# Moving weight preparation to other visits, and the first expert splits and products into attention, in a fused attention and two-expert kernel

## The chip, the core and the metric

The kernel runs on one core of a Trainium2 chip. TensorE (PE in the profile) multiplies matrices and loads its stationary operand on a track of its own (PEld), VectorE (DVE), ScalarE (ACT) and GpSimd (POOL) work on tiles, and SyncE (SP) issues most of the DMAs. Each engine runs its own instructions in the order in which the program hands them over. The metric is the device time of one execution in microseconds; lower is better.

## What is computed

The inputs are 4 batches of 8 heads, 576 positions, head size 64. Attention with a decay bias gives 2304 tokens of 512 numbers, and two dense experts follow, one behind the other.

```
scores = scale * q @ k.T + min(-(cum_i - cum_j), 0), causal      # cum: running sum of max(s, 0)
attn   = exp(scores - max) / (sum + 1e-9)
x      = attn @ v, as 2304 x 512
h      = max(x @ w_in, 0);        x = (h * h) @ w_out             # w_in 512 x 2048
h      = max(x @ w1, x @ w2, x @ w3);  out = h @ w_out            # w1, w2, w3 512 x 768
```

All of it is float32. The experts get the precision out of products of a shorter type: each operand is split into a high and a low part, and each product is made as three (high x high, high x low, low x high).

## The kernel before

**Attention** runs over 16 head pairs with 9 units each (units 0 to 143; N is 144). A loop over steps n emits, at each step, one stage of several units: ORDER lists the stages with their distances. Scores (u_s, two steps ahead) go to PSUM, u_max (L531, DVE) takes the row maximum, u_exp (L545, ACT) the exponential, u_t (L590, L597, PE) transposes blocks and the row sums into a PSUM tile, w_cp (L556, L558, DVE) takes reciprocals of the sums, u_et (L617 to L622, ACT) copies the blocks out, w_pv (L642, PE) multiplies by v, w_out_ (L653, DVE) copies the result to xT, and w_px (L658, POOL) scales it by the reciprocals, which take a way through DRAM. A head pair has two windows: w_pv is called for the first with units 0 to 3, for the second with units 4 to 8.

**The changeover.** The first products of the first expert are already made in attention. first_split(kk) splits a quarter of the first 512 tokens (ACT makes the high part, L665, DVE the low part, L666), for kk of 0 to 3 at steps 136, 138, 140 and 142. first_products makes 2 x 12 products (L672) into two PSUM banks ("first", which take the place of the tile "pair") at 3 per step from step 144 on, between the stages of the last units. Then experts() splits the same 512 tokens once more into its own tiles xs, and starts.

**The experts** run over tokens in chunks. The first expert has nine visits: chunks 0 to 3 (512, 512, 512, 384 tokens) with the first 8 of 16 blocks of the hidden size (visits 0 to 3), chunk 4 (384) with all 16 (visit 4), and chunks 3, 2, 1, 0 with the other 8 (visits 5 to 8). main1 lists its steps: a step "h" makes 12 products for a block (L672), whose result ACT and DVE turn into a split hidden block (L777 ACT, L778 DVE, L780 ACT, L781 DVE), and a step "x" two blocks later multiplies that by w_out into four PSUM banks with 12 products (L798). At the end of a visit the four banks are copied out (L808 DVE for two of them, L810 ACT), and in visits 0 to 3 stored to DRAM as partial sums. The next visit takes the same four banks one step later. Splits xs of the next visit's tokens are made in the last steps of a visit. The second expert follows in 6 chunks of 384 (L838, L879).

**Weights.** There are 56 weight tiles: 32 of the first expert ("in", "out"), 24 of the second (18 "w", 6 "out2"). Each must be prepared by a job (w_job): two loads on SP, DVE instructions L340, L344, L348, L351, (L355), a high part on ACT (L360) and a low part on DVE (L363, for which adder says GpSimd or DVE; in the experts L355 and L363 are DVE's). The class Slots plans the jobs: pump() is called once per step, advances open jobs, and starts one if a weight is needed soon (SOON) or if the pace allows. There are 24 slots in SBUF. Tiles of the second expert may also be prepared early ("early"): with no slot the job's result goes to a tile "spare", is stored to DRAM (keep, L366, SP), and is fetched into a slot 6 steps before its use by a DMA of GpSimd's queue (w_bring, L379). Early jobs begin only from step 80 (EARLY_FROM), in the middle of visit 4, and no faster than one in PACE_EARLY 2.4, counted in steps of 512 tokens.

**The plan that comes out.** By steps of main1 (a visit of 8 blocks is 16 steps; visit 4 is steps 62 to 93 with its last products at step 97), jobs begin at steps 1 to 25, one in two steps; none from 26 to 62, when all slots are taken; then "in" 13 to "out" 15 from 63 to 79, then 8 "w" tiles straight into slots from 81 to 98, and 16 early jobs from 102 to 149. The 16 kept tiles are fetched at steps 162 to 183.

Of the kernel before, what the change touches and what calls it, by code (L numbers as in the profile page):

```python
# [9 lines left out]
F32R = mybir.dt.float32r  # L10
# [3 lines left out]
ALU = mybir.AluOpType  # L14
# [4 lines left out]
HELD_BACK = 3  # L19
# [3 lines left out]
PUMP_FROM = 9  # L23
PUMP_END = 0
PRE = 2
PRE_X = 8
PRE_AT = 0
PRE_N = 3
PUMP_U = (0, 2, 3, 4, 5, 7)
WA_BUFS = 3  # L30
DELAY_ATT = (2, 6, 2, 2, 2, 2, 4, 0, 1, 1)
# [3 lines left out]
SOON = 6  # L35
SOON_KEPT = 6
PACE_EARLY = 2.4
EARLY_FROM = 80
RR = 2
LAG = 2  # L40
MAX_OPEN = 3
# [39 lines left out]
class Slots:  # L81
# [8 lines left out]
    def __init__(self, steps, make, bring, early, room):  # L90
        self.steps = steps
        self.uses = {}
        for n, ids in enumerate(steps):
            for i in ids:
                self.uses.setdefault(i, []).append(n)
        self.make, self.bring, self.early, self.room = make, bring, early, dict(room)
        self.free = []
        self.held = {}
        self.open = []
        self.kept = set()  # L100
        self.coming = set()
        self.pos = 0
        self.clock = 0.0
        self.last = -100.0
        self.pace = PACE_ATT
        self.delays = DELAY_ATT
        self.most = ADV_ATT
        self.idle_from = None

    def add(self, tiles):  # L110
        self.free += tiles
# [52 lines left out]
    def start(self):  # L164
        for n in range(self.pos, len(self.steps)):
            for i in self.steps[n]:
                if i in self.held or i in self.coming:
                    continue
                kept = i in self.kept
                if n - self.pos > (SOON_KEPT if kept else SOON) and (kept or self.clock - self.last < self.pace):  # L170
                    return False
                if not kept and not self.can_open():
                    return False
                if not self.free and not self.evict(n):
                    return False
                self.fill(i)
                return True
        return False

    def pump(self, time):  # L180
        self.clock += time
        done = 0
        for job in list(self.open):
            while job in self.open and self.clock >= job.ready and done < self.most:
                if not self.step(job):
                    break
                done += job.at > 2
        if not self.start() and self.idle_from is not None and self.pos >= self.idle_from and \
                self.clock - self.last >= PACE_EARLY and self.can_open():
            going = [job.i for job in self.open]  # L190
            i = next((i for i in self.early if i not in self.held and i not in self.kept and i not in going), None)
# [23 lines left out]
def kernel(  # L215
# [15 lines left out]
    nc = tc.nc  # L231
    P = 128
    D = v_tail.shape[2]
    S = qT.shape[2]
# [17 lines left out]
    def f32(ap):  # L252
        return ap.bitcast(F32)
# [406 lines left out]

    three = ((0, 0), (0, 1), (1, 0))

    def split_x(t0, n, kk, high, low):
        src = xT[:, kk, t0:t0 + n]
        nc.scalar.copy(out=high[:, 0:n], in_=src)  # L665
        nc.vector.tensor_tensor(out=low[:, 0:n], in0=src, in1=f32(high[:, 0:n]), op=ALU.subtract)  # L666
        return high, low

    def h_products(hps, x, n, w):
        for kk in range(KD):  # L670
# [5 lines left out]

    first_x = {}

    def first_split(kk):
        if kk < HELD_BACK:  # L680
            high, low = (slots_a[-1 - kk][:, i, :] for i in range(2))
        else:
            high, low = (hp.tile([P, S], F32R, tag=n, name=n)[:, 0:512] for n in ("xk", "xq"))
        first_x[kk] = split_x(*chunks1[0], kk, high, low)

    def first_products():
        for m in range(PRE):
# [2 lines left out]
    def attention():  # L690
# [10 lines left out]
        for n in range(-span, N + span + 1):  # L701
# [10 lines left out]
            for op, d in ORDER:  # L712
# [8 lines left out]
                        wfn[op](*wins[n + d])  # L721
                elif 0 <= n + d < N:
                    fns[op](n + d)
            if n == N:
                phQ.close()
                banks.extend(psum(ctx, "first", 2, [P, 512]))
            if PRE and n >= N - PRE_X and (n - N + PRE_X) % 2 == 0 and (n - N + PRE_X) // 2 < KD:
                first_split((n - N + PRE_X) // 2)
            if n >= N - PRE_AT:
                for _ in range(PRE_N):  # L730
                    next(pre, None)
# [3 lines left out]
    def experts():  # L735
# [2 lines left out]

        slots.delays, slots.most, slots.pace = DELAY, ADV, PACE
        adder[0] = nc.vector  # L740
        slots.idle_from = EARLY_FROM
        slots.add(slots_a[-HELD_BACK:] + [sl_p.tile([P, 2, 512], F32R, name=f"slb{i}") for i in range(SLOTS_B)])

        def xsplit(t0, n, kk):
# [209 lines left out]
```

## Time and profile before

| | us |
|---|---|
| time, median of 3 runs (lowest, highest) | 896.93 (896.42, 897.15) |
| the profiled execution's own time | 896.98 |
| its span, first to last instruction | 895.2 |
| PE busy | 855.9 (96%) |
| DVE busy | 514.3 (57%) |
| ACT busy | 332.2 (37%) |
| POOL busy | 66.9 (7%) |

The profile is of one execution. The 1.8 us between its time and its span lie outside of the instructions. Attention takes up to about 179 us, the first expert from there to about 580, the second up to the end. A busy PE is 96% of the span as the profile models it; where the products of a stretch stand at their even pitch, only a shorter program would help, and where a row shows idle time before it, something was late.

### The profile page before, as it was taken

The numbers are of one execution on the slowest core, as the hardware profiler recorded it, in microseconds if no ns is written. First come the engines' busy times: TensorE is split into PE (matmuls) and PEld (weight loads), VectorE is DVE, ScalarE is ACT, GpSimd is POOL, SyncE is SP. The second block draws the span as 40 slices with busy tenths as digits, with TensorE's granted clock in tenths as the row PEclk, the third lists the DMA queues.
The fourth block names the chain that finished last, engine by engine and source line by source line (L and its number), as shares of the span: only waits on it lengthen the run. The fifth ranks groups of instructions, "written<-read, shape, count | busy, mean of one in ns | idle before, by whom it ended". The sixth has DMA issues, their size and how long they took to land.

```text
span 895.2 us, 14075 instructions
## 1 busy us (share of the span) xinstructions
PE 855.9 (96%) x5446; PEld 730.0 (82%) x5446; DVE 514.3 (57%) x1079; ACT 332.2 (37%) x729; POOL 66.9 (7%) x79
## 2 busy tenths in 40 slices
PE   5999888899899999998999999999999999999998
PEld 3555555577688899997998888899999999999997
DVE  6788797868886333788888777633223131312211
ACT  5788887843333223323333333311112120212111
POOL 2133333310000000000000000110000000000000
PEclk9999999999999999999999999999999999999999
DMA  4454545212321020432425355950000000000001
GB/s 144 152 151 126 177 125 166 86 57 94 125 88 47 1 83 1 142 95 94 130 69 196 116 190 184 318 151 1 13 24 1 36 1 36 1 25 12 12 24 36
DMA packets 45267, 79.00 MB, mean 88 GB/s; under 512 B 7568, under 2 KB 17360, under 8 KB 45200
## 3 DMA queue, kind: packets, MB, share of 16 engines
q1 hardware_dynamic: 42884, 69.70, 24.3%
q0 software_dynamic: 2304, 8.39, 3.1%
q8 instruction: 43, 0.70, 0.3%
q14 instruction: 24, 0.20, 0.1%
q10 hardware_dynamic: 12, 0.01, 0.0%
HBM read 60.84 MB, written 17.22 MB: 87 GB/s over the span
## 4 chain that ended last, share of the span: by engine, by line
PE 75%; DVE 14%; ACT 6%; issue 4%; DMA 1%; DVEq 0%; ACTq 0%
PE banks L838 17%; PE banks L798 16%; PE first L838 8%; PE banks L879 8%; PE first L672 8%; PE banks L672 8%; PE pairs L642 4%; PE pairs L590 3%; DVE e L531 2%; PE pair L508 2%; DVE st L351 2%; PE pairs L508 2%; DVE r L778 2%; ACT hh L780 2%; ACT et L619 2%
## 5 line engine op out<-in xcount | busy, mean ns | idle before, releaser
L798 PE MATMUL banks<-hh,sl 128*128 128x512 f32 (+1 forms) x840 | 187.1, 371 | 4.4 <-DVE pt L808 1.8
L798 PEld LDWEIGHTS banks<-hh,sl 128*128 128x128 f32 x840 | 153.9, 189 | 27.7 <-DVE pt L808 2.2
L838 PE MATMUL banks<-xs,sl 128*128 128x384 f32 x720 | 128.7, 334 | 0.0
L838 PEld LDWEIGHTS banks<-xs,sl 128*128 128x128 f32 x720 | 125.1, 188 | 0.0
L780 ACT CAST hh<-r 128x512 fp32r<-128x512 f32 (+1 forms) x80 | 46.2, 578 | 152.8 <-DVE r L778 152.8
L672 PE MATMUL banks<-xs,sl 128*128 128x512 f32 (+1 forms) x420 | 92.0, 367 | 0.0
L672 PE MATMUL first<-xs,sl 128*128 128x512 f32 (+1 forms) x396 | 87.2, 368 | 4.4 <-DVE xs L666 3.2
L545 ACT ACTIVATE e<-e,nm 128x128 f32<-128x128 f32 (+2 forms) x144 | 83.5, 582 | 11.9 <-DVE nm L531 11.5
L672 PEld LDWEIGHTS banks<-xs,sl 128*128 128x128 f32 x420 | 76.7, 188 | 9.9
L672 PEld LDWEIGHTS first<-xs,sl 128*128 128x128 f32 x396 | 72.3, 188 | 13.9 <-DVE xs L666 3.5
L781 DVE TENSOR_TENSOR hh<-r,hh 128x512 fp32r<-128x512 f32 (+1 forms) x80 | 51.1, 639 | 51.5 <-ACT hh L780 50.2
L854 DVE TENSOR_TENSOR r<-banks,r 128x384 f32<-128x384 f32 x54 | 30.1, 557 | 78.5 <-PE banks L838 78.0
L879 PE MATMUL banks<-sl,hh 128*128 128x512 f32 (+1 forms) x342 | 74.9, 378 | 0.0
L879 PEld LDWEIGHTS banks<-sl,hh 128*128 128x128 f32 x342 | 61.8, 188 | 11.8
L858 ACT CAST hh<-r 128x384 fp32r<-128x384 f32 x36 | 18.5, 513 | 138.4 <-DVE r L854 138.4
L590 PEld LDWEIGHTS pairs<-identF,e 64*128 64x128 f32 x800 | 33.4, 139 | 30.6 <-ACT et L619 23.2
L590 PE MATMUL pairs<-identF,e 64*128 64x64 f32 x800 | 41.4, 230 | 16.8 <-ACT et L619 16.5
L642 PEld LDWEIGHTS pairs<-et,xv 128*64 128x64 f32 (+1 forms) x448 | 27.8, 135 | 31.2 <-ACT e L545 8.3
L642 PE MATMUL pairs<-et,xv 128*64 128x320 f32 (+4 forms) x448 | 52.7, 367 | 0.0
L838 PE MATMUL first<-xs,sl 128*128 128x384 f32 x288 | 52.0, 335 | 0.0
L838 PEld LDWEIGHTS first<-xs,sl 128*128 128x128 f32 x288 | 50.3, 188 | 0.5
L854 DVE TENSOR_TENSOR r<-first,r 128x384 f32<-128x384 f32 x18 | 10.0, 558 | 67.3 <-PE first L838 67.3
(104 smaller groups left out, 1116.1 us busy)
## 6 DMA issues: line engine op xcount, KB each, us to landing
st<-in_w_out_dram SPq DMA_DIRECT2D x44, 256.0 KB
st<-in_w_dram SPq DMA_DIRECT2D x36, 256.0 KB
st<-in_w_in_dram SPq DMA_DIRECT2D x32, 256.0 KB
keep_w<-spare SPq DMA_DIRECT2D x10, 512.0 KB
xk<-in_kT_dram SPq DMA_DIRECT2D x16, 288.0 KB
xq<-in_qT_dram SPq DMA_DIRECT2D x16, 288.0 KB
out_dram<-ob SPq DMA_DIRECT2D x17, 256.0 KB
xv<-in_v_main_dram SPq DMA_DIRECT2D x16, 256.0 KB
```

The lines of the kernel that those rows point to most:

```text
L508: nc.tensor.matmul(b[:, j, 0:w], lhsT=d["xq"][rows(j), w - P:w], rhs=d["xk"][rows(j), 0:w], start=True, stop=False)
L545: nc.scalar.activation(out=e_u[u][:, 0:w], in_=e_u[u][:, 0:w], func=ACTF.Exp, scale=-1.0, bias=st.pop(n), accum_out=sums[p, win][:, col:co ...
L590: nc.tensor.transpose(t[:, h, at * D:(at + 1) * D], e_u[v][rows(h), k * P:(k + 1) * P], identF[rows(h), rows(h)])
L642: nc.tensor.matmul(pv[rows(j), f:(W0, W1)[w]], lhsT=xv[0:kr, j, k, :], rhs=rhs, start=(k == 0), stop=(k == last))
L672: nc.tensor.matmul(hps[:, 0:n], lhsT=w[:, wp, kk * P:(kk + 1) * P], rhs=x[kk][xp][:, 0:n], start=(kk == 0 and c == 0), stop=(kk == KD - 1 ...
L780: nc.scalar.copy(out=hh[:, 0, 0:n], in_=r[:, 0:n])
L781: nc.vector.tensor_tensor(out=hh[:, 1, 0:n], in0=r[:, 0:n], in1=f32(hh[:, 0, 0:n]), op=ALU.subtract)
L798: nc.tensor.matmul(xacc[d][:, 0:n], lhsT=w[:, wp, d * P:(d + 1) * P], rhs=hh[:, xp, 0:n], start=(m == 0 and c == 0), stop=(end and c == 2))
L838: nc.tensor.matmul(pj[j][:, 0:n], lhsT=w[:, wp, kk * P:(kk + 1) * P], rhs=xs[kk][xp][:, 0:n], start=(kk == 0 and c == 0), stop=(kk == KD - ...
L854: nc.vector.tensor_tensor(out=r[:, 0:n], in0=p[:, 0:n], in1=r[:, 0:n], op=ALU.max)
L858: nc.scalar.copy(out=hh[:, 0, 0:n], in_=r[:, 0:n])
L879: nc.tensor.matmul(po[:, 0:hi - lo], lhsT=hs[ci, f][:, hp_, t * P:(t + 1) * P], rhs=w[:, wp, lo:hi], start=(c == 0), stop=(c == 3 * NF2 - 1))
```

## The change

The change does four things.

- Early jobs may begin in any step but those of visits 0, 1 and 4 (EARLY_NOT_IN); before, from step 80 on. As the plan comes out, 8 early jobs ("w" 0,0 to 1,2) now begin at steps 36 to 59, in visits 2 and 3; "in" 13 to "out" 15 stay at 63 to 79; no job begins from 80 to 93; 16 early jobs begin at 94 to 143. So all 24 tiles of the second expert go through DRAM (24 stores and 24 fetches, before 16), and the fetches begin at step 154.
- Weights that are needed more than 24 steps ahead (FAR) are begun at PACE_FAR 3 rather than 1.5: at steps 12, 15, 18, ... 33 rather than 11, 13, 15, ... 25.
- The four first splits move to steps 114, 123, 132 and 139 (PRE_X 30, 21, 12, 5), and the DVE half of each comes one step behind its ACT half.
- The first products begin at step 143 rather than 144 (PRE_AT 1), 5 per step rather than 3.

```diff
-PRE_X = 8
-PRE_AT = 0
-PRE_N = 3
+PRE_X = (30, 21, 12, 5)
+PRE_AT = 1
+PRE_N = 5
...
-EARLY_FROM = 80
+EARLY_NOT_IN = (0, 1, 4)
+FAR = 24
+PACE_FAR = 3
...
-                if n - self.pos > (SOON_KEPT if kept else SOON) and (kept or self.clock - self.last < self.pace):
+                pace = self.pace if n - self.pos <= FAR else max(self.pace, PACE_FAR)
+                if n - self.pos > (SOON_KEPT if kept else SOON) and (kept or self.clock - self.last < pace):
                     return False
...
-        if not self.start() and self.idle_from is not None and self.pos >= self.idle_from and \
+        if not self.start() and self.pos in self.idle and \
                 self.clock - self.last >= PACE_EARLY and self.can_open():
...
-    def first_split(kk):
-        if kk < HELD_BACK:
-            high, low = (slots_a[-1 - kk][:, i, :] for i in range(2))
-        else:
-            high, low = (hp.tile([P, S], F32R, tag=n, name=n)[:, 0:512] for n in ("xk", "xq"))
-        first_x[kk] = split_x(*chunks1[0], kk, high, low)
+    def first_split(kk, low):
+        if not low:
+            if kk < HELD_BACK:
+                first_x[kk] = tuple(slots_a[-1 - kk][:, i, :] for i in range(2))
+            else:
+                first_x[kk] = tuple(hp.tile([P, S], F32R, tag=n, name=n)[:, 0:512] for n in ("xk", "xq"))
+        (high if not low else low_of)(*chunks1[0], kk, *first_x[kk])
...
-            if n == N:
+            if n == N - PRE_AT:
                 phQ.close()
                 banks.extend(psum(ctx, "first", 2, [P, 512]))
-            if PRE and n >= N - PRE_X and (n - N + PRE_X) % 2 == 0 and (n - N + PRE_X) // 2 < KD:
-                first_split((n - N + PRE_X) // 2)
+            for kk in range(KD):
+                for later in range(2):
+                    if n == N - PRE_X[kk] + later:
+                        first_split(kk, later)
...
-        slots.idle_from = EARLY_FROM
+
+        slots.idle = set(range(len(steps)))
+        for i, step in enumerate(main1):
+            if step[1] in EARLY_NOT_IN:
+                slots.idle.discard(i)
```

The new functions high and low_of are the two halves of split_x.

PE at the end of attention, before: the 24 first products (L672) stand in portions of 3, 9 and 12, the last of them behind the last product with v (L642).

```order
L672 MATMUL first_2787<-sl_86,sl_67 128x512 x3
L590 MATMUL pairs_90<-identF,e_154 128x64 x10
L597 MATMUL pairs_90<-identF,sm_2698 5x64 x2
L672 MATMUL first_2787<-sl_85,sl_67 128x512 x3
L672 MATMUL first_2787<-sl_84,sl_67 128x512 x3
L672 MATMUL first_2787<-xk,sl_67 128x512
L672 MATMUL first_2787<-xq,sl_67 128x512
L672 MATMUL first_2787<-xk,sl_67 128x512
L642 MATMUL pairs_91<-et_2757,xv 64x320 x6
L642 MATMUL pairs_91<-et_2757,xv 64x192 x2
L642 MATMUL pairs_91<-et_2757,xv 64x64 x2
L672 MATMUL first_2788<-sl_86,sl_68 128x512 x3
```

PE there after the change (L672 has become L680, L642 L645); five products already stand ahead of the 16 transposes that come before these rows, and five more end and begin around the ten transposes.

```order
L680 MATMUL first_2767<-xk,sl_67 128x512
L593 MATMUL pairs_90<-identF,e_154 128x64 x10
L600 MATMUL pairs_90<-identF,sm_2703 5x64 x2
L680 MATMUL first_2767<-xq,sl_67 128x512
L680 MATMUL first_2767<-xk,sl_67 128x512
L680 MATMUL first_2768<-sl_86,sl_68 128x512 x3
L680 MATMUL first_2768<-sl_85,sl_68 128x512 x3
L680 MATMUL first_2768<-sl_84,sl_68 128x512 x3
L680 MATMUL first_2768<-xk,sl_68 128x512
L680 MATMUL first_2768<-xq,sl_68 128x512
L680 MATMUL first_2768<-xk,sl_68 128x512
L645 MATMUL pairs_91<-et_2757,xv 64x320 x6
```

All 24 first products now stand ahead of the last product with v, which was ahead of 12 of them.

DVE at the end of visit 4, before: up to the copies of the visit's banks (L808), job instructions stand between the hidden blocks (L778, L781).

```order
L778 SCALAR_TENSOR_TENSOR r<-first_2787,r 128x384
L781 TENSOR_TENSOR hh<-r,hh 128x384
L363 TENSOR_TENSOR sl_78<-wa,sl_78 128x512
L340 TENSOR_SCALAR wa<-st 128x512
L344 SCALAR_TENSOR_TENSOR st<-st,wa 128x512
L348 TENSOR_SCALAR wa<-st 128x512
L351 SCALAR_TENSOR_TENSOR st<-st,wa 128x512
L355 TENSOR_TENSOR wa<-st 128x512
L778 SCALAR_TENSOR_TENSOR r<-first_2788,r 128x384
L781 TENSOR_TENSOR hh<-r,hh 128x384
L340 TENSOR_SCALAR wa<-st 128x512
L344 SCALAR_TENSOR_TENSOR st<-st,wa 128x512
```

DVE there after the change (L778 has become L793, L808 L823, L666 L670).

```order
L793 SCALAR_TENSOR_TENSOR r<-first_2768,r 128x384
L796 TENSOR_TENSOR hh<-r,hh 128x384
L793 SCALAR_TENSOR_TENSOR r<-banks_2865,r 128x384
L796 TENSOR_TENSOR hh<-r,hh 128x384
L670 TENSOR_TENSOR xs<-xT,xs 128x384 x2
L793 SCALAR_TENSOR_TENSOR r<-banks_2866,r 128x384
L796 TENSOR_TENSOR hh<-r,hh 128x384
L793 SCALAR_TENSOR_TENSOR r<-first_2767,r 128x384
L796 TENSOR_TENSOR hh<-r,hh 128x384
L793 SCALAR_TENSOR_TENSOR r<-first_2768,r 128x384
L796 TENSOR_TENSOR hh<-r,hh 128x384
L823 COPY xT<-banks_2868 128x384
```

No job instruction is left in the last six hidden blocks ahead of the copies.

DVE at the end of visit 0, before: ahead of the two copies of the visit's banks (L808).

```order
L363 TENSOR_TENSOR sl_82<-wa,sl_82 128x512
L348 TENSOR_SCALAR wa<-st 128x512
L351 SCALAR_TENSOR_TENSOR st<-st,wa 128x512
L355 TENSOR_TENSOR wa<-st 128x512
L340 TENSOR_SCALAR wa<-st 128x512
L344 SCALAR_TENSOR_TENSOR st<-st,wa 128x512
L778 SCALAR_TENSOR_TENSOR r<-first_2788,r 128x512
L781 TENSOR_TENSOR hh<-r,hh 128x512
L363 TENSOR_TENSOR sl_83<-wa,sl_83 128x512
L348 TENSOR_SCALAR wa<-st 128x512
L351 SCALAR_TENSOR_TENSOR st<-st,wa 128x512
L355 TENSOR_TENSOR wa<-st 128x512
```

DVE there after the change.

```order
L366 TENSOR_TENSOR sl_82<-wa,sl_82 128x512
L343 TENSOR_SCALAR wa<-st 128x512
L347 SCALAR_TENSOR_TENSOR st<-st,wa 128x512
L351 TENSOR_SCALAR wa<-st 128x512
L354 SCALAR_TENSOR_TENSOR st<-st,wa 128x512
L358 TENSOR_TENSOR wa<-st 128x512
L793 SCALAR_TENSOR_TENSOR r<-first_2768,r 128x512
L796 TENSOR_TENSOR hh<-r,hh 128x512
L823 COPY pt<-banks_2868 128x512
L823 COPY pt<-banks_2870 128x512
L366 TENSOR_TENSOR sl_83<-wa,sl_83 128x512
```

From the start of the first expert up to the copies, six job instructions fewer stand in DVE's queue, which is one job's worth; the low part of "in" 8 (sl_83) has come behind the copies.

## Rows read from the trace of the kernel before

**Rows 1.** Stretches: us; busy (instructions) of PE, PEld, DVE, ACT, POOL; PEclk, DMA share, GB/s.

```profile
300.00:320.00 20.00, 20.00 (x93) 16.96 (x92) 6.39 (x10) 5.69 (x10) 0.00 (x0) 1.00 0.00 0
400.00:420.00 20.00, 17.70 (x101) 17.01 (x99) 17.27 (x33) 6.42 (x14) 0.00 (x0) 1.00 0.25 87
```

**Rows 2.** Timeline of PE around 416: start us, us, engine, line, count [idle before <-releaser].

```profile
416.06 1.20 PE L672 MATMUL first<-xs,sl 128*128 128x384 f32 x6
...
422.06 1.48 PE L672 MATMUL first<-xs,sl 128*128 128x384 f32 x5 [3.20 <-DVE xs L666]
...
426.70 2.24 PE L672 MATMUL first<-xs,sl 128*128 128x384 f32 x12
428.78 2.24 PE L798 MATMUL banks<-hh,sl 128*128 128x384 f32 x12
...
436.64 2.24 PE L672 MATMUL banks<-xs,slb 128*128 128x384 f32 x12
```

**Rows 3.** Timeline of DVE, the splits that PE waited for.

```profile
421.46 1.02 DVE L666 TENSOR_TENSOR xs<-xT,xs 128x384 fp32r<-128x384 f32 x2
```

**Rows 4.** A short stretch, columns as in rows 1.

```profile
422.00:426.00 4.00, 3.94 (x14) 3.94 (x15) 3.35 (x8) 1.42 (x3) 0.00 (x0) 0.58 0.29 102
```

**Rows 5.** DVE by line and form, 345 to 470 us: busy us, mean ns | idle before.

```profile
L781 DVE TENSOR_TENSOR hh<-r,hh 128x384 fp32r<-128x384 f32 x26 | 14.5, 559 | 15.1 <-ACT hh L780 15.1
L351 DVE SCALAR_TENSOR_TENSOR st<-st,wa 128x512 f32<-128x512 uint32 x18 | 12.5, 694 | 0.6
...
L340 DVE TENSOR_SCALAR wa<-st 128x512 uint32<-128x512 uint32 x18 | 7.6, 421 | 0.0
```

**Rows 6.** Timeline of PE at the end of visit 0.

```profile
236.41 2.88 PE L672 MATMUL banks<-xs,sl 128*128 128x512 f32 x12
239.13 0.92 PE L798 MATMUL banks<-hh,sl 128*128 128x512 f32 x3
...
243.98 2.20 PE L672 MATMUL banks<-xs,sl 128*128 128x512 f32 x9
```

**Rows 7.** Timeline of DVE at the end of visit 0, the two copies.

```profile
241.07 1.28 DVE L808 COPY pt<-banks 128x512 f32<-128x512 f32 x2
```

**Rows 8.** Timeline of PE, last head pairs.

```profile
157.34 0.71 PE L590 MATMUL pairs<-identF,e 64*128 64x64 f32 x16 [1.20 <-ACT et L619]
...
170.87 0.28 PE L590 MATMUL pairs<-identF,e 64*128 64x64 f32 x2 [0.37 <-ACT e L545]
171.78 1.13 PE L508 MATMUL pairs<-xk,xq 64*128 64x512 f32 x4 [0.64 <-DVE nm L531]
```

**Rows 9.** Timeline of DVE, the first of the four splits.

```profile
170.45 0.93 DVE L666 TENSOR_TENSOR sl<-xT,sl 128x512 fp32r<-128x512 f32 x1 [0.76 <-ACT sl L665]
```

**Rows 10.** Timeline of PE at the changeover.

```profile
180.16 0.71 PE L590 MATMUL pairs<-identF,e 64*128 64x64 f32 x16 [1.54 <-ACT et L619]
180.80 0.96 PE L672 MATMUL first<-sl,sl 128*128 128x512 f32 x3
181.69 0.52 PE L590 MATMUL pairs<-identF,e 64*128 64x64 f32 x10
...
184.47 2.42 PE L642 MATMUL pairs<-et,xv 128*64 128x320 f32 x20
...
193.17 2.79 PE L798 MATMUL banks<-hh,sl 128*128 128x512 f32 x11 [0.23 <-DVE hh L781]
```

**Rows 11.** Timeline of DVE at the changeover.

```profile
187.01 0.49 DVE L653 COPY xT<-pairs 128x320 f32<-128x320 f32 x1 [3.44 <-PE pairs L642]
187.41 3.72 DVE L666 TENSOR_TENSOR xs<-xT,xs 128x512 fp32r<-128x512 f32 x4
...
192.43 0.69 DVE L781 TENSOR_TENSOR hh<-r,hh 128x512 fp32r<-128x512 f32 x1 [0.69 <-ACT hh L780]
```

**Rows 12.** Line L658, 184 to 192 us: durations min/median/max, first and last start.

```profile
L658 POOL TENSOR_TENSOR xT<-xT,px x3: 870/917/1033, 184.8 to 189.7; 128x320 f32<-128x320 f32 x2, 128x256 f32<-128x256 f32 x1
```

**Rows 13.** A stretch of the fetches, columns as in rows 1.

```profile
560.00:580.00 20.00, 20.00 (x90) 16.54 (x90) 14.21 (x24) 6.28 (x12) 4.22 (x8) 1.00 1.00 330
```

More of the change, by code (lines that the diff above doesn't have):

```diff
@@ L107, in __init__ @@
         self.most = ADV_ATT
-        self.idle_from = None
+        self.idle = ()
     def add(self, tiles):
@@ L661, with high, low_of, split_x @@
     three = ((0, 0), (0, 1), (1, 0))
[L663 to L667, printed above, removed]
+    def high(t0, n, kk, hi, lo):
+        nc.scalar.copy(out=hi[:, 0:n], in_=xT[:, kk, t0:t0 + n])
+    def low_of(t0, n, kk, hi, lo):
+        nc.vector.tensor_tensor(out=lo[:, 0:n], in0=xT[:, kk, t0:t0 + n], in1=f32(hi[:, 0:n]), op=ALU.subtract)
+    def split_x(t0, n, kk, hi, lo):
+        high(t0, n, kk, hi, lo)
+        low_of(t0, n, kk, hi, lo)
+        return hi, lo
     def h_products(hps, x, n, w):
```

## The prediction, as it was put on record

> **What bounds the kernel now.** I read the 20-us stretches first. In the experts PE is busy all the time in most of them [rows 1]; the exceptions are what a plan can give back. So I went to the timeline of PE and compared the pitch of its steps. Undisturbed, a step of 12 products takes 2.08 us with 384 tokens (428.78 to the row before it, [rows 2]) and 2.72 us with 512 (236.41 to 239.13, [rows 6]), 0.227 us for one product. Three places fall out of that pitch.
>
> The largest is the end of visit 4: from 416.06 to 436.64 PE gets through six steps in 20.58 us, where six at 2.08 are 12.48. So 8.1 us are lost there [rows 2]. Its longest wait is 3.20 us for DVE's splits of the next visit's tokens, which DVE reached at 421.46 [rows 3]. DVE was not waiting for anyone; it was busy 17.27 of 20 us in that stretch, and its rest is the pause of each hidden block between L778 and L781, 15.1 us for 26 blocks [rows 1, 5]. A part of the 8.1 us is clock: after PE had been nearly idle, the granted clock was 0.58 in the next 4 us, a mix of the two levels 1.2 and 2.4 GHz [rows 4]. The six steps include that, and the wait for the copies at the visit's end.
>
> The second is the end of visit 0: a step begins at 239.13 and the next at 243.98, 4.85 us instead of 2.72, so 2.1 us are lost [rows 6]. DVE came to the copies of the visit's banks only at 241.07 [rows 7]; the products wait for them.
>
> The third is the end of attention, where PE waits 0.9 to 1.5 us in each head pair for a copy of ACT, which stands behind DVE's sums (1.20 and 1.54 us, [rows 8, 10]).
>
> **Part 1, the early jobs (weights).** One job costs DVE four instructions like L351 at 0.69 us and two like L340 at 0.42: 3.6 us [rows 5]. A hidden block of 384 tokens costs L778 and L781 at about 0.56 each and the pause of 0.58: 1.7 us [rows 5]. Before, jobs begin from step 63 at one per 2.25 steps, 4.7 us of PE: 3.6 + 1.125 x 1.7 = 5.5 us of DVE by these sums. DVE falls behind by up to 0.8 us a job, and some 14 jobs lie ahead of the splits and copies at the visit's end. After, 8 of them begin, the last at step 79, and their last instruction stands at step 86; then 11 steps or 23 us follow with only hidden blocks (six at 1.7 us, 10 us) and the splits, and a lag of 8 x 0.8 = 6.4 us is worked off there. So the whole 8.1 us should go, the slow clock with them. Bounds: 5 us if some lag is left, 8.1 if none; I take 8.1, as the order shows no job instruction among the last six blocks.
>
> The moved jobs go to visits 2 and 3, where DVE was busy 6.39 of 20 us [rows 1]. There they come one in three steps: with 512 tokens 8.2 us of PE against 3.6 + 1.5 x 2.1 = 6.7 of DVE (a block of 512 is three times 0.69, [rows 11]); with 384 tokens 6.2 against 3.6 + 1.5 x 1.7 = 6.2 for three jobs, then one in four steps. I followed DVE's queue instruction by instruction over the two visit ends concerned (steps 49 and 65): the copies come some 1.5 to 2 us ahead of the step that needs them. So I cost them at nothing, with that little cover. On SP each job adds a store that waits for DVE's low part, with the loads of the next job behind it; the loads are issued 3 steps ahead, as they are now in visits 6 to 8, where no step of PE is late. The 8 stores and 8 fetches more are 8 x 0.52 MB each way (128 x 1024 numbers of 4 bytes); the fetches of steps 154 to 161 go at one per 2.72 us, 193 GB/s, where 330 were moved [rows 13].
>
> **Part 2, the slower pace.** By the end of visit 0 one job less has been handed to DVE: 3.5 us off ahead of the copies. They would be reached some 3.5 us earlier against PE, 2.1 us are needed, and the wait goes: 2.1 us (bounds 1.0 and 2.1). The jobs of "out" 5 and 6 begin in the same steps, so the two shorter waits for their weights in visit 0 stay.
>
> **Part 3, the changeover.** I call X the end of the last head pair's first product with v (178.6, where the wait of 1.54 us begins). From there PE has 16 transposes, 12 first products and 10 transposes up to 184.47, so 4.31 us from 180.16, and the last product with v follows [rows 10]. After, all 24 products are ahead of it: 4.31 + 12 x 0.227 = 7.03, and a third portion, which costs some 0.2 us (three products take 0.89 instead of 0.68, 180.80 to 181.69). The wait of 1.54 is filled by the first five (1.3 us). So it starts at X + 7.2 instead of X + 5.9: 1.3 us later. PE has nothing to lose by that, but DVE has: its copy L653 follows that product, in order behind it come four splits (3.72 us), and only then the first hidden block, for which PE waits until 193.17 [rows 10, 11]. From 187.41 to 241.07 DVE has no pause but those of the blocks, so what it gets late there it keeps: PE's two waits in visit 0 hang on it too. I therefore charge the 1.3 us in full. It would be nothing only if DVE had slack, which these rows exclude; a gain needs X to come earlier.
>
> X itself: three of the low splits now stand between u_max and the reciprocals of a head pair, on the chain that ends PE's wait of 1.20 us [rows 8]. Each is 0.69 to 0.93 us long [rows 9]; bounds 0 and 2.1 us for the three, I take 1.6, since ACT waits for that reciprocal today. The last head pair loses the waits of 0.37 and 0.64 us that its splits caused (DVE stood 0.76 us for ACT, [rows 8, 9]): -1.0; bounds -1.7 (0.76 + 0.93) and -0.6. So X comes 0.6 us later, and the changeover costs 1.3 + 0.6 = 1.9 us, with bounds -0.4 and 2.8.
>
> Four splits take 3.72 us there, 0.93 each, while GpSimd's products L658 run [rows 11, 12]. The Trainium skill, SBUF — State Buffer, section "Who interferes with whom", says that a VectorE instruction with two SBUF inputs contends with a GpSimd instruction that reads SBUF. By that rule the splits would take about 0.69 each if the products no longer met them, and the forecast would be 1.0 us lower. The trace agrees so far that they stretch; the products would move by about as much as the splits, so I leave the 3.72.
>
> **The sum.** 896.98 (the profiled execution's own time; the median is 896.93) - 8.1 - 2.1 + 1.9 = 888.7 us. By the bounds of the parts: 896.98 - 10.2 - 0.4 = 886.4 and 896.98 - 5.0 - 1.0 + 2.8 = 893.8, if all bad ends meet.
>
> **The rivals.** (B) The changeover pays. If PE's own stream set the experts' start, the wait of 1.54 and the two of the last pair would go and the added splits would be hidden: -2.5 instead of +1.9, so 884.3. For it: PE stands still in each head pair. Against it: DVE is without slack from 187 on.
> (C) The waits move to visits 2 to 4. The cover at steps 49 and 65 is 1.5 to 2 us, and visit 4 begins with jobs in flight. If one job's 3.6 us more lie ahead of the copies than I count, DVE is 3.6 - 1.75 late at each of the two ends: 888.7 + 3.7 = 892.4. Against it: DVE's sums stay under PE's up to step 63.
> (D) Slower: fetches too late. The second expert now takes 18 "w" tiles in a row, one per 2.08 us, each 0.52 MB, so 252 GB/s; 330 were moved at full share [rows 13]. The six steps of lead cover 12.5 us. If only 140 GB/s came through, a tile would take 3.7 us, the last would be 18 x 1.66 = 30 us late, less the cover 17: 906. It turns the gain into a loss below about 160 GB/s. Against it: ten in a row already come with no gap on PE. The Trainium skill, SBUF — State Buffer, section "SBUF: two separate sides", warns that a DMA of GpSimd's queue can wait for its descriptors while VectorE holds the shared port, 620 ns becoming about 3100. By that a tile would take 3.1 us, the last would be 6 us late, and the time 894.6; the trace shows no sign, as the eight records of POOL there take 0.53 us each beside a DVE that is busy 14.21 of 20 us [rows 13].
> (E) The change does not do it: something else holds the splits at visit 4's end, and only part 2 and 3 count: 896.98 - 2.1 + 1.9 = 896.8. Against it: PE's row names DVE, and DVE has no idle time before 421.46.
>
> **How the numbers follow.** Forecast 0.66, B 0.12, C 0.13, D 0.04, E 0.05. The range 885.5 to 893.0 holds the forecast with its bounds and C, and leaves out most of B, D and E, 0.2 at most. A measurement of this kernel tells a difference of about 0.2% (1.8 us) from none: faster by more than that is the forecast, B and C (0.91), within it E (0.05), slower D (0.04).
>
> **What would show it.** Right: no step of PE over 2.3 us from the end of visit 4 to step 99, clock at 1.0 there; no wait for the copies at visit 0's end; DVE about 15 of 20 us busy in visits 2 and 3; last product with v about 7.2 us behind X, and PE waiting over 1 us for the splits in front of the first hidden block. Wrong: PE idle at the ends of visits 1 to 3; PE waiting for a fetch at the start of the second expert; DVE with idle time between 190 and 230.

## The result, and the profile of the changed kernel

| | us |
|---|---|
| after, median (lowest, highest), 4 runs | 888.41 (886.56, 890.20) |
| before, beside it, 4 runs | 897.04 (896.42, 898.99) |
| ratio (95% interval) | 0.990 (0.9873 to 0.9927) |
| after, the profiled execution's own time; its span | 887.58; 885.8 |
| forecast | 888.7 (885.5 to 893.0) |

The change makes the kernel 1.0% faster, and the forecast holds. The profiled execution is 9.4 us under the one of before (896.98). Its page begins with the busy time of each engine (share of the span, instructions):

```profile
PE 854.1 (96%) x5446; PEld 728.9 (82%) x5446; DVE 514.7 (58%) x1079; ACT 334.0 (38%) x729; POOL 72.1 (8%) x87
```

PE and DVE are as busy in all as before; the span is shorter because PE stands still less. At the end of visit 4, where [rows 2] had steps out of pitch, the timeline of PE shows one step of 12 products after the other, each 2.08 or 2.09 us behind the last:

```profile
415.52 2.24 PE L680 MATMUL first<-xs,sl 128*128 128x384 f32 x12
417.61 2.24 PE L813 MATMUL banks<-hh,sl 128*128 128x384 f32 x12
419.69 2.24 PE L680 MATMUL first<-xs,sl 128*128 128x384 f32 x12
421.76 2.24 PE L813 MATMUL banks<-hh,sl 128*128 128x384 f32 x12
423.85 2.24 PE L680 MATMUL banks<-xs,sl 128*128 128x384 f32 x12
```

DVE's timeline there (what answers to [rows 3]) has the splits 8.8 us earlier, and now it is DVE that waits, for PE's results through ACT. Its first wait for a new block ends at 410.07, 5 us behind the last job instruction. The copies of the visit's banks (L823) follow without a job between them and the last hidden block:

```profile
404.29 0.70 DVE L366 TENSOR_TENSOR sl<-wa,sl 128x512 fp32r<-128x512 f32 x1
...
410.07 0.56 DVE L793 SCALAR_TENSOR_TENSOR r<-banks,r 128x384 f32<-128x384 f32 x1 [1.40 <-ACT r L792]
...
412.63 1.08 DVE L670 TENSOR_TENSOR xs<-xT,xs 128x384 fp32r<-128x384 f32 x2 [0.86 <-ACT xs L667]
...
422.55 0.56 DVE L793 SCALAR_TENSOR_TENSOR r<-first,r 128x384 f32<-128x384 f32 x1 [2.46 <-ACT r L792]
423.69 0.56 DVE L796 TENSOR_TENSOR hh<-r,hh 128x384 fp32r<-128x384 f32 x1 [0.58 <-ACT hh L795]
424.16 1.01 DVE L823 COPY xT<-banks 128x384 f32<-128x384 f32 x2
```

The stretches by windows (us; busy of PE, PEld, DVE, ACT, POOL; granted clock, DMA share, GB/s) answer to [rows 1] and [rows 4]. The moved jobs are seen as DVE's 15.28 of 20 us where it was 6.39; 17.27 has become 11.20 in front of the visit's end; the clock is 1.00 behind it, where it was 0.58; and the fetches of the second expert move 253 GB/s in a stretch in which PE has no idle time:

```profile
300.00:320.00 20.00, 20.00 (x94) 17.04 (x92) 15.28 (x27) 7.26 (x13) 0.00 (x0) 1.00 0.31 105
400.00:420.00 20.00, 20.00 (x117) 20.00 (x116) 11.20 (x21) 7.31 (x15) 0.00 (x0) 1.00 0.13 42
424.00:428.00 4.00, 4.00 (x25) 4.00 (x24) 2.92 (x7) 1.60 (x5) 0.00 (x0) 1.00 0.00 0
540.00:560.00 20.00, 20.00 (x90) 16.56 (x89) 14.87 (x25) 5.95 (x11) 2.93 (x6) 1.00 0.83 253
```

At the end of visit 0 the steps of PE stand at 2.72 us (238.09, 240.81, 243.53), and the copies of the banks on DVE come at 239.44, ahead of the products that need them (PE's timeline, then DVE's); [rows 6] and [rows 7] had 4.85 us and a copy that came too late:

```profile
238.09 2.88 PE L680 MATMUL banks<-xs,sl 128*128 128x512 f32 x12
240.81 2.88 PE L813 MATMUL banks<-hh,sl 128*128 128x512 f32 x12
```

```profile
239.44 1.28 DVE L823 COPY pt<-banks 128x512 f32<-128x512 f32 x2
```

The changeover, PE (what answers to [rows 10]): the last product with v starts at 186.25, and now there are waits in front of the first hidden block, for DVE's splits and for the block itself:

```profile
178.97 1.42 PE L680 MATMUL first<-sl,sl 128*128 128x512 f32 x5
...
186.25 2.42 PE L645 MATMUL pairs<-et,xv 128*64 128x320 f32 x20
188.60 0.50 PE L680 MATMUL banks<-xs,sl 128*128 128x512 f32 x1
190.41 1.66 PE L680 MATMUL banks<-xs,sl 128*128 128x512 f32 x6 [1.31 <-DVE xs L670]
192.29 1.42 PE L680 MATMUL banks<-xs,sl 128*128 128x512 f32 x5 [0.23 <-DVE xs L670]
194.15 0.51 PE L813 MATMUL banks<-hh,sl 128*128 128x512 f32 x1 [0.43 <-ACT hh L795]
194.88 2.33 PE L813 MATMUL banks<-hh,sl 128*128 128x512 f32 x9 [0.22 <-DVE hh L796]
```

**Where the 9.4 us went.** PE comes back at the first hidden block at 194.88 instead of 193.17: +1.7. Visit 0's end: -2.1. Visit 4's end: -8.1, the slow clock included. That makes -8.5; the last product ends 8.6 us earlier than before (882.70 and 891.33), so all but 0.1 is named. Behind the last product the span goes on for 3.09 us, before for 3.88: -0.8. No step of the prediction covers it. ACT's last copy into the output tile (ob) shows where it comes from: before, it waited for the landing of an earlier store (`DMA out_dram<-ob`) and started 0.80 us behind the last product; after, it waits only for that product and starts 0.03 us behind it. The timeline of ACT, before and then after:

```profile
892.13 0.37 ACT L886 COPY ob<-banks 128x256 f32<-128x256 f32 x1 [8.57 <-DMA out_dram<-ob]
```

```profile
882.73 0.37 ACT L901 COPY ob<-banks 128x256 f32<-128x256 f32 x1 [7.80 <-PE banks L894]
```

In the ten other traces with the new plan this copy waits for the product too, and the tail is 3.09 to 3.11 us; in the one with the old plan it waits for the store, and the tail is 3.68. Why that store lands later under the old plan stays open.

### The profile page after: what moved, and what is told of

It reads as the page before. It is cut to its first block, busy times and chain, and to the rows that moved or that the text cites. A ratio compares the mean times of both kernels' runs of the same rounds, so it can differ in the third digit from the quotient of the medians.

```text
span 885.8 us, 14109 instructions
## 1 busy us (share of the span) xinstructions
PE 854.1 (96%) x5446; PEld 728.9 (82%) x5446; DVE 514.7 (58%) x1079; ACT 334.0 (38%) x729; POOL 72.1 (8%) x87
## 4 chain that ended last, share of the span: by engine, by line
PE 87%; DVE 7%; ACT 4%; issue 2%; DMA 1%; DVEq 0%; ACTq 0%
PE banks L813 20%; PE banks L853 17%; PE first L680 10%; PE banks L680 10%; PE first L853 8%; PE banks L894 8%; PE pairs L645 4%; PE pairs L593 3%; PE pair L511 2%; DVE e L534 2%; PE pairs L511 2%; ACT et L622 1%; ACT et L620 1%; ACT e L548 1%; DVE xs L670 1%
## 5 line engine op out<-in xcount | busy, mean ns | idle before, releaser
L813 PE MATMUL banks<-hh,sl 128*128 128x512 f32 (+1 forms) x840 | 185.0, 368 | 2.0 <-ACT sl L363 1.2
L680 PE MATMUL banks<-xs,sl 128*128 128x512 f32 (+1 forms) x420 | 92.7, 368 | 1.5 <-DVE xs L670 1.5
L680 PEld LDWEIGHTS banks<-xs,sl 128*128 128x128 f32 x420 | 76.5, 188 | 12.1 <-DVE xs L670 2.3
L680 PE MATMUL first<-xs,sl 128*128 128x512 f32 (+1 forms) x396 | 86.3, 366 | 0.0
L680 PEld LDWEIGHTS first<-xs,sl 128*128 128x128 f32 x396 | 72.2, 188 | 9.0
L593 PE MATMUL pairs<-identF,e 64*128 64x64 f32 x800 | 41.4, 230 | 15.9 <-ACT et L622 15.9
L645 PEld LDWEIGHTS pairs<-et,xv 128*64 128x64 f32 (+1 forms) x448 | 27.8, 135 | 31.2 <-ACT e L548 8.9
L645 PE MATMUL pairs<-et,xv 128*64 128x320 f32 (+4 forms) x448 | 52.7, 367 | 0.0
L792 ACT ACTIVATE r<-first 128x512 f32<-128x512 f32 (+1 forms) x40 | 22.2, 554 | 73.8 <-PE first L680 73.3
```

The lines of the kernel that those rows point to most:

```text
L593: nc.tensor.transpose(t[:, h, at * D:(at + 1) * D], e_u[v][rows(h), k * P:(k + 1) * P], identF[rows(h), rows(h)])
L645: nc.tensor.matmul(pv[rows(j), f:(W0, W1)[w]], lhsT=xv[0:kr, j, k, :], rhs=rhs, start=(k == 0), stop=(k == last))
L680: nc.tensor.matmul(hps[:, 0:n], lhsT=w[:, wp, kk * P:(kk + 1) * P], rhs=x[kk][xp][:, 0:n], start=(kk == 0 and c == 0), stop=(kk == KD - 1 ...
L792: nc.scalar.activation(out=r[:, 0:n], in_=hps[:, 0:n], func=ACTF.Relu)
L813: nc.tensor.matmul(xacc[d][:, 0:n], lhsT=w[:, wp, d * P:(d + 1) * P], rhs=hh[:, xp, 0:n], start=(m == 0 and c == 0), stop=(end and c == 2))
```

## The experiments

Theory: the gain is DVE's lag alone. Jobs in the second half of visit 4 put DVE behind PE, and one job too many in visit 0 does the same there; the changeover gives some of it back, by a late last product with v. Rivals: the waits were for something else than the jobs (E of the prediction), or the changeover costs nothing or pays (B). Times are medians; "before" is the kernel before on the same chip, run in between.

| kernel | us | before | ratio (95% interval) |
|---|---|---|---|
| new plan, old changeover | 886.94 | 898.61 | 0.9876 (0.9859 to 0.9892) |
| the same again | 886.29 | 898.77 | 0.9861 (0.9842 to 0.9880) |
| old plan, new changeover | 898.69 | 898.61 | 1.0007 (0.9995 to 1.0019) |
| the whole change again | 886.97 | 898.43 | 0.9878 (0.9860 to 0.9896) |
| the whole change, third | 888.25 | 898.77 | 0.9885 (0.9865 to 0.9906) |
| without the slower pace | 891.63 | 898.61 | 0.9924 (0.9901 to 0.9946) |
| early jobs also in visit 4 | 888.53 | 898.43 | 0.9892 (0.9874 to 0.9911) |
| the same, at a fast pace | 895.63 | 898.43 | 0.9968 (0.9955 to 0.9980) |
| product with v ahead of 12 products | 884.19 | 898.61 | 0.9850 (0.9830 to 0.9869) |
| the same again | 884.55 | 898.77 | 0.9844 (0.9823 to 0.9866) |
| the same, splits one step later | 884.10 | 898.43 | 0.9845 (0.9827 to 0.9863) |

Each execution is recorded with its mean granted clock, 1.000 to 0.992 in the runs of this table. A stretch of 4 us at 0.57 costs about 1.7 us (4 x 0.43, an estimate) and 0.002 of that mean, so kernels are also compared at the same clock below. The mean is a rough guide only: one execution of the first set took 890.20 with a mean of 0.970, which by this rate would have cost some 25 us and did not.

**The two halves apart.** The plan alone:

```diff
-PRE_X = (30, 21, 12, 5)
-PRE_AT = 1
-PRE_N = 5
+PRE_X = (8, 6, 4, 2)
+PRE_AT = 0
+PRE_N = 3
...
-                    if n == N - PRE_X[kk] + later:
+                    if n == N - PRE_X[kk]:
```

> Only the new plan of the weight jobs (early jobs out of visits 0, 1 and 4, slower pace for far weights); splits and first products of attention as before the change. My theory (DVE's chain behind the last product with v sets the experts' start, and the moved changeover costs 1.7 us): 888.4 - 1.7 = 886.7, PE back at the first hidden block at 193.2 us as before. Rival (the moved changeover gains, since it fills PE's waits in the last head pair): about 890 to 891, later than after the whole change. Rival (the two parts only work together): the waits at the ends of visits 0 and 4 are still there in part, 890 or more.

The changeover alone:

```diff
-                pace = self.pace if n - self.pos <= FAR else max(self.pace, PACE_FAR)
+                pace = self.pace
...
-        for i, step in enumerate(main1):
-            if step[1] in EARLY_NOT_IN:
-                slots.idle.discard(i)
+        slots.idle -= set(range(80))
```

> Only the moved splits and first products; the plan of the weight jobs as before the change. My theory: 897.0 + 1.7 = 898.7, the waits at 240 and 418 us are there, 1.7 us later. Rival (the moved changeover gains): 894.5 to 896.

The plan alone took 886.94 and has neither of the two long waits; the changeover alone took 898.69 and has both. So the gain is the plan's. The changeover's cost did not show as clearly. The plan alone is 1.5 us under the 888.41 of the whole change, as expected, but level with 886.97, the whole change on another chip; and 898.69 stands beside 898.61, where 1.7 us more were expected. One reason is in the stretch from 180 to 184 us of the plan alone (columns as in the windows above):

```profile
180.00:184.00 4.00, 4.00 (x34) 2.78 (x33) 1.18 (x3) 2.32 (x5) 0.00 (x0) 0.57 0.14 46
```

The old changeover has the wait of 1.55 us ahead of the transposes, and in this execution half clock came right behind it; in the trace of before the same stretch has 1.00. That made a new pair of theories: the changeover costs what was forecast but spares PE the wait and with it the half clock (theory 1 in the next texts), or it costs less at full clock too (theory 2). Three kernels on one chip were to tell:

> The changed plan with the changeover of before once more, beside the changed kernel, to measure the changeover by itself. Theory 1 (the changeover costs 1.9 us at full clock, as forecast, but the old one has a wait of 1.55 us ahead of the transposes of the last window which in most executions is followed by half clock, at 1.6 us): executions with a mean clock of 1.000 take 884.5 to 885.3, those with 0.998 take 886.3 to 887.2; median within 0.6 us of the changed kernel's. Theory 2 (the changed changeover costs less than forecast at full clock too): executions with a mean clock of 1.000 stand within 0.6 us of the changed kernel's with a clock of 1.000. The trace is to show granted clock 0.5 to 0.65 from 180 to 184 us where its own mean is 0.998.

> The changed kernel as it is, on the same chip as the kernel with the changed plan alone: 886.3 to 887.6 with a mean clock of 0.999 to 1.000, up to 890 with a lower one. Theory 1: its executions at clock 1.000 are 1.3 to 1.9 us above those of the changed plan alone at 1.000. Theory 2: the same within 0.6 us.

The plan alone: 885.60 and 885.50 where the clock was 1.000, 886.99 and 887.15 where it was 0.998. The whole change: 886.95, 888.38 and 888.13 at 1.000, 888.96 at 0.998. By these few executions the changeover costs 2.3 us at full clock (885.55 against the mean 887.82) and 2.0 us in the medians. The plan alone was caught at 1.000 this time; its timeline of PE:

```profile
180.59 0.71 PE L593 MATMUL pairs<-identF,e 64*128 64x64 f32 x16 [1.55 <-ACT et L622]
...
184.90 2.42 PE L645 MATMUL pairs<-et,xv 128*64 128x320 f32 x20
...
190.12 2.88 PE L680 MATMUL banks<-xs,sl 128*128 128x512 f32 x12
192.84 2.91 PE L813 MATMUL banks<-hh,sl 128*128 128x512 f32 x12
```

There is no wait left in front of the hidden block. Counted from the end of the last pair's first product with v (X, 180.59 - 1.55 = 179.04), its second product with the hidden block stands 14.0 us behind (192.84 + 0.23), in the changed kernel 15.9 (194.88 - 178.97), in its third trace 15.75. So theory 1 holds in the main: the changeover costs 1.7 to 1.9 us against the plan alone. Its numbers were not all met: the whole change was expected at 886.3 to 887.6 at full clock, at most 1.9 us above the plan alone there, and the medians within 0.6. The old changeover pays 0.9 to 1.5 us for half clock in most executions (of the eight of the plan alone three had the mean 1.000 and five 0.998). Against the old plan the numbers fit, less sharply: at the mean clock 0.996 the changeover alone took 899.8 to 900.4, before 896.0 to 899.1.

The new changeover has a risk of the same kind elsewhere. The moved splits lengthen the wait at 158 us from 1.20 to 1.82 us (shown below), and in two of the nine traces that have this longer wait a stretch of half clock follows it, at a cost of some 1.5 us. One of them, from the kernel with the fast pace below:

```profile
160.00:164.00 4.00, 4.00 (x32) 2.34 (x32) 2.83 (x10) 3.15 (x11) 0.73 (x1) 0.64 0.17 53
```

**The parts of the plan.** Without the slower pace:

```diff
-                pace = self.pace if n - self.pos <= FAR else max(self.pace, PACE_FAR)
+                pace = self.pace
```

> The whole change without the slower pace for weights that are needed more than 24 steps ahead. My theory (one job more stands ahead of the copies at the end of visit 0, where DVE has no slack): the wait of 2.1 us at about 242 us returns, 888.4 + 2.1 = 890.5. Rival (the wait went because the moved changeover shifts DVE and PE against each other): no wait there, 888.4. Early jobs then begin at step 30 rather than 36, at the same pace, which neither theory charges.

The wait at the end of visit 0 is back, and with it a half clock that the trace of before does not have behind the same wait ([rows 6]; there the stretch from 244 to 248 us has 1.00). Timeline of PE, and then the stretch:

```profile
241.68 0.89 PE L813 MATMUL banks<-hh,sl 128*128 128x512 f32 x3
244.32 3.91 PE L813 MATMUL banks<-hh,sl 128*128 128x512 f32 x9 [1.76 <-DVE pt L823]
```

```profile
244.00:248.00 4.00, 3.68 (x9) 2.96 (x10) 3.28 (x7) 1.44 (x3) 0.00 (x0) 0.58 0.73 235
```

2.0 us of wait and some 1.6 of clock, 3.6 in all, lie within the 3.2 to 4.7 us by which 891.63 is over the medians of the whole change; the one execution at 1.000 took 888.84, which is 0.5 to 2.5 over those of the whole change. By the trace the pace is worth about its forecast 2.1, and more where the clock falls.

Early jobs also in visit 4, as the plan's other half undone, at the pace as it is and then at a fast one:

```diff
-EARLY_NOT_IN = (0, 1, 4)
+EARLY_NOT_IN = (0, 1)
```

> The whole change, but early jobs may begin in visit 4 too, at the pace that they have elsewhere: three jobs begin at steps 83, 87 and 91. Theory with the lag of the prediction (6.4 us at step 80): 14 steps of 2.08 us are 29 us, DVE's work in them 3 x 3.6 + 7 x 1.7 + four splits 2.2 = 25, so 2 to 3 us of lag are left at the visit's end and PE waits 1 to 2 us: 889.5 to 890.5. If the lag at step 80 is only 2 to 3 us, it is worked off and nothing comes back: 888.4.

```diff
-EARLY_NOT_IN = (0, 1, 4)
+EARLY_NOT_IN = (0, 1)
...
-                self.clock - self.last >= PACE_EARLY and self.can_open():
+                self.clock - self.last >= (1.5 if 62 <= self.pos < 94 else PACE_EARLY) and self.can_open():
```

> The whole change, but in visit 4 early jobs may begin and as fast as one per 1.5 (two steps): five jobs are added there, at steps 62, 84, 86, 88 and 92. My theory (DVE's lag at the end of visit 4 makes the wait, and the lag is the sum of its job instructions): five jobs of 3.6 us against about 12 us of slack bring 5 to 6 us of lag back, PE waits for the splits at the start of visit 5 and the clock falls behind it: 888.4 + 6 to 8 = 894 to 896. Rival (the wait hung on the loads or on one job's place in the queue): under 890.

Three jobs (steps 83, 87 and 91) bring back one wait of 0.50 us for the splits, where 1 to 2 us were expected. 888.53 is 1.6 us over the 886.97 of the whole change on that chip; the rest of it is not shown to be the jobs', and the profiled execution (889.86) has lost 1.5 us at 160 us, as above. Five (steps 62, 84, 86, 88 and 92) bring back most of it: 895.63, with 894 to 896 expected. Of the latter the timeline of PE, that of DVE, and two stretches:

```profile
417.10 1.20 PE L680 MATMUL first<-xs,sl 128*128 128x384 f32 x6
419.06 0.44 PE L680 MATMUL first<-xs,sl 128*128 128x384 f32 x1 [0.77 <-ACT xs L667]
422.70 1.97 PE L680 MATMUL first<-xs,sl 128*128 128x384 f32 x5 [3.20 <-DVE xs L670]
...
434.48 1.86 PE L813 MATMUL banks<-hh,sl 128*128 128x384 f32 x9 [0.44 <-DVE xT L823]
436.18 2.24 PE L680 MATMUL banks<-xs,slb 128*128 128x384 f32 x12
```

```profile
420.42 0.69 DVE L358 TENSOR_TENSOR wa<-st 128x512 f32<-128x512 f32 x1
421.03 0.42 DVE L343 TENSOR_SCALAR wa<-st 128x512 uint32<-128x512 uint32 x1
421.49 0.69 DVE L347 SCALAR_TENSOR_TENSOR st<-st,wa 128x512 uint32<-128x512 uint32 x1
422.10 1.02 DVE L670 TENSOR_TENSOR xs<-xT,xs 128x384 fp32r<-128x384 f32 x2
```

```profile
400.00:420.00 20.00, 18.74 (x107) 18.16 (x105) 17.30 (x33) 7.00 (x16) 0.00 (x0) 1.00 0.21 70
424.00:428.00 4.00, 4.00 (x21) 4.00 (x20) 3.41 (x6) 1.47 (x4) 0.00 (x0) 0.79 0.33 133
```

The row of 422.70 is that of [rows 2] again, with the same 3.20, the splits stand behind job instructions as in [rows 3], DVE is at 17.30 of 20 us, and the clock falls. The six steps from 417.10 to 436.18 take 19.08 us where 12.48 is their pitch, so 6.6 of the 8.1 us are back here; 895.63 is 8.7 over 886.97, but this execution too has the 1.5 us at 160 us, which the edit does not touch. This is the experiment that settles the cause: the jobs' place alone, with the changeover and the rest of the code as in the changed kernel, makes the wait and its slow clock.

**Scatter.** The whole change on another chip:

> The kernel after the change once more, as the base of this group. All theories: about 1% faster than before on the same chip; a profile with its waits at 189 to 195 us and two at 222 to 231 us, and no step of PE out of its pitch behind those.

886.97 there and 888.25 on a third: the kernel's median moves by some 1.4 us from set to set.

**A better place for the product with v.** By the prediction's own step the 1.3 us come from all 24 first products standing ahead of it. With five of them at each of two steps, two at a third, and then none until it has passed, it stands ahead of 12 again:

```diff
-                for _ in range(PRE_N):
+                for _ in range({N - 1: 5, N: 5, N + 1: 2, N + 2: 0, N + 3: 0}.get(n, 5)):
```

> The whole change, but the last product with v stands behind the first 12 of the 24 first products rather than behind all. My theory (DVE's chain copy, four splits, first hidden block sets the start): the copy L656 comes about 2.7 us earlier (12 products at 0.227), PE is at the first hidden block at 192.2 instead of 194.9, and all behind it moves: 885.7. Rival (PE's own stream sets the start): no change, 888.4. Rival (the splits' ACT halves wait for a DMA that lands at 186.6): about half of it, 887.0.

> The changed kernel with the last product with v behind 12 of the 24 first products, on the same chip once more: 883.8 to 884.5, so 2.5 to 3.5 us under the changed kernel. By theory 1 it also stands under the changed plan alone at clock 1.000 by 0.5 to 1.5 us; by theory 2 by 2 us or more.

884.19 and 884.55, under both kernels, and 3.7 us under the whole change on the same chip. Against the plan alone there it is 1.7 us in the medians and some 1.7 at a clock of 1.000 (883.52 and 884.18 against 885.55), which lies between what theory 1 (0.5 to 1.5) and theory 2 (2 or more) had for it. PE of the first of the two:

```profile
183.35 2.42 PE L645 MATMUL pairs<-et,xv 128*64 128x320 f32 x20 [0.43 <-ACT et L625]
185.70 2.33 PE L680 MATMUL first<-sl,sl 128*128 128x512 f32 x9
...
188.56 2.88 PE L680 MATMUL banks<-xs,sl 128*128 128x512 f32 x12
191.28 2.88 PE L813 MATMUL banks<-hh,sl 128*128 128x512 f32 x12
```

No wait in front of the hidden block, and, as in the changed kernel, none ahead of the transposes of the last window. It gained more than expected, because the four splits too became shorter. The line's durations (min/median/max in ns), of the changed kernel and then of this one:

```profile
L670 DVE TENSOR_TENSOR xs<-xT,xs x4: 678/922/1359, 189.2 to 192.2; 128x512 fp32r<-128x512 f32 x4
```

```profile
L670 DVE TENSOR_TENSOR xs<-xT,xs x4: 681/683/684, 186.3 to 188.1; 128x512 fp32r<-128x512 f32 x4
```

Last, the low halves of the first splits one step later still, so that they stand behind the reciprocals (with the edit above):

```diff
-                    if n == N - PRE_X[kk] + later:
+                    if n == N - PRE_X[kk] + 2 * later:
```

> The product with v behind 12 of the 24 first products, and the DVE half of each split one step later still, behind the reciprocals rather than ahead of them. My theory (each of three splits lengthens the chain that ends PE's wait, 1.4 us in all): the waits at 145, 156 and 168 us are 1.1, 1.2 and 0.9 us as before the change, and the time is 1.2 us under that with the product moved alone (884.2): 883.0. Rival (the split then delays the next maximum, and PE waits for the exponential instead): 884.2 to 885.

The waits of PE ahead of the transposes are back to the length of before, 1.20 and 0.90 us instead of 1.82 and 1.18, and the traces stand 0.7 us apart (883.19 and 883.90 for the profiled executions). The medians, 884.10 on one chip and 884.19 and 884.55 on two others, can't tell that from nothing, so the 1.2 us expected are not shown. PE waits for no exponential there, so the rival's mechanism did not come either.

## Why the prediction was right

**Visit 4 (-8.1).** Right in size and mechanism, the bound "none left" and not the 5 us. The lag itself was put somewhat high: DVE's first pass over a block (L793) stands 2.86 us behind the start of the block's products where DVE has waited for it (422.55 and 419.69), and at 402.64 it stood 7.91 us behind them (394.73), so the lag was about 5.1 us at its largest (an estimate), where 6.4 were forecast. The margin is small: three jobs brought one wait of 0.50 us back, five at a fast pace 6.6 us.

**Visit 0 (-2.1).** Right: the copies begin at 239.44, the first ends some 0.7 us later, and the product that needs it starts 0.68 us (three products) behind 240.81. The prediction could not see the second price of that wait, a half clock that follows it in some executions.

**Cover at the ends of visits 2 and 3.** No wait came, so rival C is out. Of the 1.5 to 2 us of cover about 1.3 is found at the end of visit 2, where DVE's copies begin at 324.62 and the fourth product of PE's step at 326.08 is the first to need them (DVE's row and PE's).

```profile
324.62 1.28 DVE L823 COPY pt<-banks 128x512 f32<-128x512 f32 x2
```

```profile
326.08 2.24 PE L813 MATMUL banks<-hh,sl 128*128 128x384 f32 x12
```

**The changeover (+1.9).** 1.3 for the product with v: right; from X it starts 7.28 us behind (forecast 7.2), and PE is back 15.9 us behind X instead of 14.55 ([rows 10]), +1.36. 0.6 for X itself: not found. At the wait ahead of the transposes at 125 us, before any moved split, the trace of after is already 0.42 us later than that of before, and X is 0.35 later; so X did not move. Of its two pieces the chain of reciprocals lost 1.25 us at two waits and 0.12 at a third (1.6 taken):

```profile
158.51 0.72 PE L593 MATMUL pairs<-identF,e 64*128 64x64 f32 x16 [1.82 <-ACT et L622]
169.71 0.71 PE L593 MATMUL pairs<-identF,e 64*128 64x64 f32 x16 [1.54 <-ACT et L622]
```

against 1.20 in [rows 8] and 0.91; the last pair became shorter by 1.4 (1.0 taken, 1.7 the bound): the waits of 0.37 and 0.64 are gone, the other 0.4 I have not followed. The forecast 1.9 is what the changeover costs against the plan alone, while the traces of before and after differ by 1.3 there: in the trace of the plan alone the four splits behind the product take 3.04 us, where before they took 3.72.

**The splits at 3.72.** The prediction let them stand, on the ground that GpSimd's products (L661 now) would move along. In the changed kernel they do (3.65), and in the second trace of the plan alone only one of GpSimd's products meets them (3.04). Where the product with v stands earlier, the splits are nearly through when GpSimd's product comes, and take 0.68 each instead of up to 1.36. A split that was lengthened by one of GpSimd's products took 0.34 to 0.68 us more in these traces. The Trainium skill, SBUF — State Buffer, section "Who interferes with whom", says that such a VectorE instruction contends with a GpSimd instruction that reads SBUF; these traces agree. The 1.0 us that the prediction gave for it (1.2 in the traces, 3.65 against 2.49) came only with the earlier product with v, not with the change.

**The sum.** 888.7 forecast against 887.58: the 1.1 us are the tail behind the last product (0.8), the changeover (0.2) and 0.1 unnamed. That the changeover comes out within 0.2 is partly luck: of its 1.7 us in the traces 0.4 stood there ahead of the first moved split, and its own part was 1.3. Rivals B, D and E are out: the changeover alone does not pay, PE waits for no fetch, and the plan alone carries the whole gain.

## What to carry to other kernels

A planner that spreads preparation evenly over steps should count it against the engine that does it, and stop early enough ahead of a stage's end for the lag to be worked off: here jobs that are free in visits 2 and 3 cost 6.6 to 8.1 us at the end of visit 4. When work is moved up to fill a wait of the busy engine, look at what it is moved in front of; here a short product, on which another engine's chain hung, was put behind 12 longer ones and the fill cost more than the wait. A wait of some 1.5 us on TensorE may cost as much again in clock, so compare executions at the same granted clock before a change is called free.

## What the runs showed of the hardware

The same wait is followed by half clock in some executions and not in others. Behind 1.55 us ahead of the transposes the granted clock was 0.57 in one trace of the plan alone and 1.00 in the other:

```profile
180.00:184.00 4.00, 3.41 (x37) 2.60 (x38) 2.12 (x4) 3.25 (x6) 0.00 (x0) 1.00 0.09 25
```

Behind the wait at the end of visit 0, which costs 2.1 us, it was 1.00 in the trace of before and 0.57 or 0.58 in two others. Behind the 1.82 us at 158 us it was below 1.00 in two traces and 1.00 in seven. Mean clocks of the kernel before were 0.992 to 0.998, and its times on three chips 896.0 to 901.0, so its one profiled execution, at 0.997, had escaped some of this. What decides it was not found.
